# Late chunks of an mLSTM and MoE kernel: a head's three f16 terms on one set of array rows, special scores in quarters, one-hot tables on GpSimd

## Chip, cores and metric

One core of a Trainium2 chip runs the whole kernel. The metric is device microseconds of one execution, the median of several runs. TensorE (PE, with its weight loads as PEld), VectorE (DVE), ScalarE (ACT), GpSimd (POOL) and SyncE (SP, which issues most of the transfers) each work through their own list of instructions in order.

## Reference

Two parts follow each other. The first is an mLSTM over 4 batches, 8 heads, 768 steps, head size 40; the second routes each of the 3072 tokens to one of 8 experts.

```python
for t in range(S):                                   # mLSTM, per batch and head
    C = f * C + i * outer(v_t, k_t);  n = f * n + i * k_t
    y_t = sigmoid(o_t) * (C @ q_t) / max(|n . q_t|, 1)
x = y as (3072 tokens, 8 heads * 40 = 320)
logits = x @ w_gate + modality_bias[modality_id]      # 8 experts
e = argmax(logits);  p = softmax(logits)[e]
out = p * (relu(x @ w1[e]) @ w2[e])                   # 320 -> 1024 -> 320
```

## The kernel before

**Chunks.** The tokens are cut into 24 chunks of 128. Chunks 0 to 21 hold tokens whose output is a product of q with one state of their batch (`S`, 40 rows by 41 columns for each head, the 41st for the denominator); chunks 22 and 23 hold the first 64 steps of each batch, which need their own scores and are called special.

- Chunks 0 to 13 multiply in f32 (`light`, the matmul on L1976): three heads lie under each other on 120 rows of the array, and the state's blocks are masked so that one matmul gives the three heads' 123 columns. Three matmuls make a chunk (3, 3 and 2 heads).
- Chunks 14 to 21 (`light16`, L1985; `SPLIT` = 7 is the first pair that goes this way) do the same in f16. q and S are each split in a high and a low part (`split_q`: ACT makes `qh` on L1983, DVE makes `ql` on L1984; `Sh` and `Sl` likewise), and each group of heads takes three matmuls on L1997: high by high, high by low, low by high. That is nine for a chunk; chunk 16 lies over two batches and has its nine twice, for 64 rows each.
- `special` (L2078): scores in f32 (L2086, 8 matmuls of 128 rows x 64 columns, with a zero-padded `sp` tile that L2470 clears), decay weights `aw` (POOL, POOL, ACT, then DVE on L2095 times the scores), then 16 matmuls with the values (L2101).

**From a chunk to a tile.** `token_rows` normalises two chunks at a time (DVE), multiplies by the reciprocal on POOL (L2034), casts on ACT and makes the low part on DVE; POOL scatters a chunk's rows to `x_s` in DRAM by an indirect transfer (L2045), ordered by modality. 14 tiles are read back transposed by SP (L2140), in the order A0, A1, A2, B0, B1, A3, B2, A4, B3, A5, B4, A6, B5, A7; a tile's transfer waits for the scatters of the chunks that can lie in it. The first three tiles are not read back but picked out of the rows by matmuls with one-hot tables (`sel`, made from positions on L2152).

**Experts.** The tokens are still (one modality, one expert), so two experts' weights, A and B, are loaded in f32 to `stage` buffers and split to f16 high (ACT, L1949) and low (DVE, L1950). A tile takes logits (L2212), a first layer (L2275, and L2283 for the last 64 of 320 rows), relu and split (`hh` on ACT L2263, `hl` on DVE L2264), a second layer (L2320) and a row-wise scatter of the output by POOL (L2341). One odd token is worked out apart: its row is fetched into `zrow` and cast by DVE (L2388).

**Order.** Each piece of work is a task. A list scheduler with a cost for each task and one nudge for each (the strings `PRIO` and `LOADS`) writes out the order on every engine, and each engine then runs strictly in this order. Where the scheduler's plan leaves PE idle for 0.25 us or more before its 60th microsecond, dummy matmuls on a zero tile `zz` are put in (L2524), sized by the planned gap.

Of the kernel before, what the change touches and what calls it, by code (L numbers as in the profile page):

```python
# [1550 lines left out]
SPLIT = 7  # L1551
# [32 lines left out]
    "{+py{Rv{'+{{QOyz{kpggTcnf)v9c_bp{g{][Y]-r,NYHJHC{YvR%%{D&bS[XMBT%5ZcR2{%fq{vtt>TO%pojs{DM7x]=J{[GX{`{acoB_{z:o"
    'Y%W{uhhvX4\\%7%{.%K.ED)2/?T4o%yg%IDCDa@_^t\\]ZyZKtss[ZniF`lgU_dc\\^{b{f{cH%{nu(%hV{%%%%YB?->kQPUX`{{uou{Bm@{zPt{{'
    "oT'{+oeab\\t4S%Z{HJ9Ctmlknn{b5{la{mjks{{ywuvlssxlkm{pRMZd4T*5J(**%<9o=e{z{{X{{yy{{vK{sxvpm{{{{V{pe{{joV%t*e%%:z"
    'mx?B%>=W8[%%h<;RQplqr{d:D]<({]%.W\\ZZig3074,?JGFd,B<o`oT9O6JKxztY{p{`{ep^{nsD{^me_\\b{*qp{ljz-h%=*wfG{2{o{R{{kXx'
    'v{^{sqswtX%ttqn{pi%?gjkuun{W{]wT{YipxSumtx^z[<tkvtseRG%Z@buec)ahrOax]GbT[al]iwmV<AOSGWUv?9%;tnfWEdb<Ca_s0]`N..'
# [63 lines left out]
def still_arm(tc, a, out):  # L1652
# [804 lines left out]
    def chunks(z):  # L2457

        for c in range(done[0], z):
            plan.early = 0.0 if c < 14 else SOON  # L2460
# [212 lines left out]
```

## Time and profile before

| what | value |
|---|---|
| median of three runs | 217.33 us (216.87 to 217.49) |
| the profiled execution: its own time | 218.61 us |
| the profiled execution: span, first to last instruction | 216.8 us |
| mean granted clock of TensorE over the span | 0.989 |

The page gives each engine's busy time over the span; the windows give it by stretch, with the granted clock (1.00 is 2.4 GHz), the DMA engines' busy share and GB/s. The timeline lists neighbouring instructions as one row with a count, and in brackets the idle time ahead of it with what ended it. Matmuls are pipelined: a matmul's listed duration is longer than the distance to the next one, so a piece of work is timed here from its start to the start of what follows.

### The profile page before, as it was taken

How to read it: one execution, taken by the hardware profiler on the slowest of the kernel's cores; microseconds unless marked ns; L12 is line 12 of the kernel's file. 1: busy time of each engine (PE TensorE's matmuls, PEld its weight loads, DVE VectorE, ACT ScalarE, POOL GpSimd, SP SyncE). 2: the span in 40 equal slices, each digit the busy share in tenths (PEclk: the TensorE clock that was granted, in tenths of full speed). 3: DMA queues.
4: the chain of work that ended last, by engine and by line, in shares of the span. 5: the costliest groups of instructions: out<-in, count | busy, mean ns of one | idle time of the engine just before them, and what ended most of it. 6: DMA issues, size and time to landing. Idle time of an engine off the chain costs nothing. (4 is left out here: it accounts for less than half of the span.)

```text
span 216.8 us, 5376 instructions
## 1 busy us (share of the span) xinstructions
PE 206.3 (95%) x2103; PEld 159.6 (74%) x2103; DVE 139.0 (64%) x447; ACT 100.4 (46%) x202; POOL 77.0 (35%) x84
## 2 busy tenths in 40 slices
PE   7899998999999999999999999999999999999970
PEld 2576786878888878878778778787787787767840
DVE  7788975597786936787806596958585159811300
ACT  3797976955655557453425242225432231322310
POOL 5040265643143653546784522330211403032021
PEclk9999999999999999999999999999999999999995
DMA  6989999294444964731637601096000880001010
GB/s 193 362 310 340 326 329 343 97 258 193 92 123 164 120 224 66 183 117 63 176 103 184 104 30 33 33 152 124 33 30 0 300 281 35 30 0 64 3 33 25
DMA packets 27115, 30.76 MB, mean 142 GB/s; under 512 B 19190, under 2 KB 19480, under 8 KB 26824
## 3 DMA queue, kind: packets, MB, share of 16 engines
q1 hardware_dynamic: 24520, 22.06, 36.8%
q0 software_dynamic: 2416, 8.13, 10.7%
q8 instruction: 18, 0.29, 0.6%
q10 hardware_dynamic: 144, 0.13, 0.2%
q14 instruction: 17, 0.14, 0.2%
HBM read 18.57 MB, written 8.22 MB: 124 GB/s over the span
## 5 line engine op out<-in xcount | busy, mean ns | idle before, releaser
L2341 POOL DMA_INDIRECT out<-ob,ois x25 | 24.7, 986 | 70.8 <-ACT ob L2336 17.5
L2320 PEld LDWEIGHTS <-hh 128*128 128x128 f16 (+1 forms) x400 | 37.8, 98 | 16.2 <-ACT hh L2263 1.1
L2264 DVE SCALAR_TENSOR_TENSOR hl<-H,hh 128x512 f16<-128x512 f32 (+2 forms) x40 | 25.8, 648 | 27.8 <-ACT hh L2263 27.7
L2263 ACT ACTIVATE hh<-H 128x512 f16<-128x512 f32 (+2 forms) x40 | 22.3, 565 | 37.5 <-PE H L2275 22.5
L2045 POOL DMA_INDIRECT x_s<-rows,pos_i x24 | 26.2, 1092 | 36.0 <-issue 5.5
L2336 ACT ACTIVATE ob<-O,zs 128x320 f32<-128x320 f32 (+1 forms) x24 | 12.5, 522 | 45.6 <-PE O L2320 32.8
L2320 PE MATMUL O<-w2hA,hh 128*128 128x320 f16 (+1 forms) x104 | 27.8, 300 | 1.0 <-ACT hh L2263 1.0
L2320 PE MATMUL O<-w2lA,hh 128*128 128x320 f16 (+1 forms) x104 | 27.8, 299 | 0.0
L2275 PE MATMUL H<-xt,w1hA 128*128 128x256 f16 (+2 forms) x176 | 26.7, 259 | 0.0
L2320 PE MATMUL O<-w2hB,hh 128*128 128x320 f16 x96 | 26.4, 299 | 0.0
L2320 PE MATMUL O<-w2lB,hh 128*128 128x320 f16 x96 | 26.4, 299 | 0.0
L2275 PE MATMUL H<-xt,w1hB 128*128 128x256 f16 x144 | 24.4, 273 | 0.0
L2320 PEld LDWEIGHTS <-hl 128*128 128x128 f16 (+1 forms) x200 | 18.9, 98 | 7.1
L2275 PEld LDWEIGHTS <-w1hA 128*128 128x128 f16 x224 | 20.3, 98 | 3.5 <-issue 1.2
L2275 PE MATMUL H<-xt,w1lA 128*128 128x256 f16 (+2 forms) x88 | 22.2, 259 | 0.0
L2275 PEld LDWEIGHTS <-w1hB 128*128 128x128 f16 x192 | 18.0, 98 | 3.1 <-issue 0.8
L2275 PE MATMUL H<-xt,w1lB 128*128 128x256 f16 x72 | 19.6, 273 | 0.0
L2034 POOL TENSOR_TENSOR xr<-xr,ab 128x640 f32<-128x640 f32 x11 | 14.5, 1318 | 9.9 <-DVE ab L2017 6.7
L2320 PE MATMUL O<-w2hA,hl 128*128 128x320 f16 (+1 forms) x104 | 16.0, 299 | 0.0
L2019 DVE SCALAR_TENSOR_TENSOR xr<-og,Y 128x320 f32<-128x320 f32 x24 | 11.3, 477 | 7.1 <-PE Y L1997 6.8
L2320 PE MATMUL O<-w2hB,hl 128*128 128x320 f16 x96 | 15.3, 299 | 0.0
L2524 PE MATMUL M<-zz 128*128 128x512 bf16 (+5 forms) x41 | 11.0, 404 | 1.1 <-DVE zz L1792 1.1
(218 smaller groups left out, 397.8 us busy)
## 6 DMA issues: line engine op xcount, KB each, us to landing
qg<-in_ql SPq DMA_DIRECT2D x11, 384.0 KB, 4.4
og<-in_ogl SPq DMA_DIRECT2D x12, 320.0 KB, 5.5
stage<-in_w1s SPq DMA_DIRECT2D x8, 320.0 KB
stage<-in_w SPq DMA_DIRECT2D x8, 320.0 KB, 3.2
stage<-in_w1t SPq DMA_DIRECT2D x1, 1280.0 KB, 8.1
og<-in_w SPq DMA_DIRECT2D x1, 1280.0 KB
kvs<-in_kvs SPq DMA_DIRECT2D x2, 364.5 KB
sp<-in_spq SPq DMA_DIRECT2D x4, 160.0 KB
```

The source lines that it names most:

```text
L2019: dve(320, lambda h=h: v.scalar_tensor_tensor(x4[:, h], og[k][:, h].rearrange("p (h d) -> p h d", h=H), 1.0, y4[h][:, :, 0:D], ALU.add, AL ...
L2034: pool(640, lambda: g_.tensor_tensor(x3, x3, ab.rearrange("p c h o -> p (c h) o").broadcast_to([P, 2 * H, D]), ALU.mult), r=abk, w=xk)
L2045: ins = g_.indirect_dma_start(out=x_s[:, :], out_offset=bass.IndirectOffsetOnAxis(ap=pos_i[:, c:c + 1].bitcast(U32), axis=0), in_=rows[:, ...
L2263: act(g * n, lambda: s_.activation(hh[:, sl, 0:n], hp3, AF.Relu), r=[nb], w=[f"hh{j}{i}" for i in fs])
L2264: dve(g * n, lambda: v.scalar_tensor_tensor(hl[:, sl, 0:n], hp3, 0.0, hh[:, sl, 0:n], ALU.max, ALU.subtract), r=[nb] + [f"hh{j}{i}" for i ...
L2275: t_.matmul(dst, lhsT=w[:, i, ws], rhs=x[:, xb], start=(first and b == 0 and q == 0), stop=(last and b == 1 and q == 2), skip_group_check= ...
L2320: t_.matmul(op[p0:p0 + nr, 0:DM], lhsT=t[:, at[f], o_:o_ + nr], rhs=w[:, f], start=(i < ways), stop=(i >= 24 - ways), skip_group_check=True)
L2336: act(z + 80, lambda op=op, o=o, qc=qc, nr=nr, z=z: s_.mul(obs[o][0:nr, 0:z], op[0:nr, 0:z], facs[0:nr, qc:qc + 1]), r=[no, f"fac{m_}"], w ...
L2341: swdma(164, lambda o=o, qc=qc, nr=nr: disjoint("outf", g_.indirect_dma_start(out=out[:, :], out_offset=bass.IndirectOffsetOnAxis(ap=ois[0 ...
L2524: t_.matmul(bank[b][:, 0:m], lhsT=zz, rhs=zz[:, 0:1].broadcast_to([P, m]), start=True, stop=True, skip_group_check=True)
```

## The change

Chunks 12 to 21 (`SPLIT` = 6) now use one matmul per head. A head's q is laid on 104 + 16 = 120 rows of the array in one f16 tile `qs`: rows 0 to 39 q high, 40 to 63 q high again, 64 to 103 q low, 104 to 119 q high again. Against them stands `SS`, whose rows 0 to 39 and 64 to 103 are the state's high part and rows 40 to 63 and 104 to 119 its low part. q comes already laid out so, one chunk at a time, by a 480 KB transfer (`in_qx`) into `stage` or `qg` buffers. `SS` is put together by 12 transfers from `Sh` and `Sl`, and those are written straight from PSUM without the mask. The scores of the special chunks are 16 matmuls of 64 x 64 on 40 rows, one for each of two row halves and two column halves of the array, into two PSUM banks. Six one-hot tables, and five small or middle operations, go from DVE to GpSimd. `PRIO` and `LOADS` are other strings; a line or two of them is shown.

```diff
-SPLIT = 7
+SPLIT = 6
+STACK = ((0, 40, 0, 0), (40, 64, 0, 1), (64, 104, 0, 0), (104, 120, 24, 1))
 PRIO = (
-    "ou^{%%vT%XKtMF3<&%6U9R{npHOM+G(&%,%%%'3.,GL9<LI[Ah%=%e>H{E%%{{{^F{%D{X6{98{J<q%sxR<{Wu%0{%Qk{%`hGEC'EG%a.?HvD8"
+    "{{*/B%gN%MVN,%O.Yqv)optC{'ZX%otsrxtxu(sjT{wy{{/%%L%%{z{f[o@O{He{OI{NvFEG{K2uFoMJ\\iNr,,{%;QoE{xi{\\`-{_u&%Fu[MXa"
...
+    def load_qx(c):
+        dma(480, lambda: sy.dma_start(qx[c % 3], a["qx"][:, c - 2 * SPLIT]), w=[f"qx{c % 3}"] + qxk[c % 3])
...
-            if S16[b]:
-                hi, lo = S16[b]
-                act(3 * HQ, lambda hi=hi, b=b: s_.mul(hi, Ss[b][0:120], SSC), r=[f"S{b % 3}"], w=[f"S{b}h"])
-                two(3 * HQ, lambda hi=hi, lo=lo, b=b: v.scalar_tensor_tensor(lo, Ss[b][0:120], SSC, hi, ALU.mult, ALU.subtract),
-                    r=[f"S{b % 3}", f"S{b}h"], w=[f"S{b}l"])
+            if pr:
+                hi, lo = (x[:, 3 * j:3 * j + 3] for x in S16)
+                act(3 * HQ, lambda hi=hi, j=j: s_.mul(hi, u3s[j][0:120], SSC), r=[ns[j]], w=[f"S{b}h"])
+                dve(3 * HQ, lambda hi=hi, lo=lo, j=j: v.scalar_tensor_tensor(lo, u3s[j][0:120], SSC, hi, ALU.mult, ALU.subtract),
+                    r=[ns[j], f"S{b}h"], w=[f"S{b}l"])
+        if pr:
+            for p0, p1, d0, x in STACK:
+                for j in range(3):
+                    k0 = D * j + d0
+                    dma(100, lambda p0=p0, p1=p1, x=x, j=j, k0=k0: sy.dma_start(SS[p0:p1, :, DV * j:DV * (j + 1)],
+                                                                             S16[x][k0:k0 + p1 - p0, :, DV * j:DV * (j + 1)]),
+                        r=[f"S{b}{'hl'[x]}" for b in (2, 3)], w=[f"SS{p0}{j}"])
...
-    def split_q(i):
-        q, (hi, lo), k, j = qg[i % 4], q16[i % 2], f"qg{i % 4}", i % 2
-        act(768, lambda: s_.mul(hi, q[0:120], QSC), r=[k], w=[f"qh{j}"])
-        two(768, lambda: v.scalar_tensor_tensor(lo, q[0:120], QSC, hi, ALU.mult, ALU.subtract), r=[k, f"qh{j}"], w=[f"ql{j}"])
-
     def light16(c, n, y):
-        if c % 2 == 0:
-            split_q(c // 2)
-        (qh, ql), i, j = q16[c // 2 % 2], c % 2, c // 2 % 2
+        k = c % 3
+        q, s = qx[k], q16[k]
+        act(1024, lambda: s_.mul(s, q, QSC), r=[f"qx{k}"], w=[f"qs{k}"])
+        two(1024, lambda: v.scalar_tensor_tensor(s[64:104], q[64:104], QSC, s[64:104], ALU.mult, ALU.subtract), r=[f"qx{k}"], w=[f"qs{k}"])

         def mm():
-            for g in range(3):
+            for h in range(H):
                 for p0, p1, b in spans(c):
-                    k, w = (120, HQ) if g < 2 else (80, 2 * DV)
-                    Sh, Sl = S16[b]
-                    for t, (a, z) in enumerate(((qh, Sh), (qh, Sl), (ql, Sh))):
-                        t_.matmul(y[p0:p1, HQ * g:HQ * g + w], lhsT=a[0:k, i, g, p0:p1], rhs=z[0:k, g, 0:w],
-                                  start=(g == 0 and t == 0), stop=(g == 2 and t == 2), skip_group_check=True)
+                    t_.matmul(y[p0:p1, DV * h:DV * h + DV], lhsT=s[:, h, p0:p1],
+                              rhs=SS[:, 3 * b - 6 + h // 3, DV * (h % 3):DV * (h % 3) + DV], start=(h == 0), stop=(h == H - 1),
+                              skip_group_check=True)
...
-    dve(24, lambda: v.tensor_copy(rows[:, :, IDC:IDC + 2].bitcast(I32).rearrange("p c o -> p (c o)"), tok_i), r=["cst"], w=["rowi"])
+    pool(24, lambda: g_.tensor_copy(rows[:, :, IDC:IDC + 2].bitcast(I32).rearrange("p c o -> p (c o)"), tok_i), r=["cst"], w=["rowi"])
...
         def scores():
             for hp in range(NP):
                 for b in range(2):
-                    t_.matmul(sc3[FT * b:FT * b + FT, 2 * hp:2 * hp + 2], lhsT=sp[:, 0, b, hp], rhs=sp[:, 1:3, b, hp],
-                              start=(hp == 0), stop=(hp == NP - 1), skip_group_check=True)
+                    for j in range(2):
+                        rs = slice(64 * j, 64 * j + D)
+                        t_.matmul(scs[j][FT * b:FT * b + FT, hp], lhsT=sp[rs, 0, b, hp], rhs=sp[rs, 1, b, hp],
+                                  start=(hp == 0), stop=(hp == NP - 1), skip_group_check=True)
...
-        dve(512, lambda: v.tensor_tensor(aw, aw, sc3, ALU.mult), r=[n], w=["aw"])
+        aw4 = aw.rearrange("p (h j) t -> p h j t", j=2)
+        for j in range(2):
+            dve(256, lambda j=j: v.tensor_tensor(aw4[:, :, j], aw4[:, :, j], scs[j], ALU.mult), r=[(n, "M0")[j]], w=["aw"])
...
-        two(selw[c] // 4 + 16, lambda: v.tensor_scalar(sels[c], iota_f[:, 0:selw[c]], float(sel0[c]), posf[:, c:c + 1], ALU.add, ALU.is_equal),
+        pool(selw[c], lambda: g_.tensor_scalar(sels[c], iota_f[:, 0:selw[c]], float(sel0[c]), posf[:, c:c + 1], ALU.add, ALU.is_equal),
...
-                load_q(c // 2) if c < 22 else None
+                load_q(c // 2) if c < 2 * SPLIT else [load_qx(x) for x in (c, c + 1)] if c < 22 else None
...
-                dve(800, lambda: v.memset(sp, 0.0), w=["spz"])
```

How the change moves instructions is seen at three places. The first is PE at one late chunk. Before, the nine f16 products of a chunk stand in the first layer of tile B1 (`H`), here the first group of heads and the beginning of the second:

```order
L2275 MATMUL H_64<-xt_108,w1lB 128x256
L1997 LDWEIGHTS qh_83
L1997 MATMUL Y_69<-Sh_87,qh_83 128x123
L1997 LDWEIGHTS qh_83
L1997 MATMUL Y_69<-Sl_88,qh_83 128x123
L1997 LDWEIGHTS ql_84
L1997 MATMUL Y_69<-Sh_87,ql_84 128x123
```

In the changed kernel a chunk is eight such pairs of load and product (here one of them, in tile B1's second layer, `O`; the seven behind it read the same):

```order
L2333 LDWEIGHTS hh0_104
L2333 MATMUL O1_67<-w2lB_96,hh0_104 128x320
L2006 LDWEIGHTS qs2_80
L2006 MATMUL Y0_69<-SS_83,qs2_80 128x41
L2006 LDWEIGHTS qs2_80
```

Each late chunk of one batch goes from nine pairs with 123 or 82 columns to eight with 41, still with a weight load of 128 columns for each.

The second place is ACT where the late chunks begin. Before, it holds one conversion of a pair of chunks (`qh`) and two of states (`Sh`) among the relu outputs `hh` of a tile:

```order
L2263 ACTIVATE hh_112<-H_63 128x512
L2333 ACTIVATE ob_116<-ob_116,zs 64x320
L1983 ACTIVATE qh_81<-qg_77 120x768
L2263 ACTIVATE hh_112<-H_64 128x512
L1876 ACTIVATE Sh_87<-S_120 120x369
L2336 ACTIVATE ob_117<-O_66,zs 128x320
L2263 ACTIVATE hh_112<-H_65 128x512
```

Now three conversions of one chunk each (`qs`, from `stage`, `qg`, `stage`) stand there, one ahead of the two states and two between the `hh`:

```order
L2000 ACTIVATE qs_79<-stage 120x1024
L1972 ACTIVATE og<-og 128x640
L1885 ACTIVATE Sh<-Y_70 120x369
L1885 ACTIVATE Sh<-Y_69 120x369
L2237 ACTIVATE ex_166<-lg_164 128x16
L2349 ACTIVATE ob_110<-O_66,zs 128x320
L2276 ACTIVATE hh_105<-H_63 128x512
L2000 ACTIVATE qs_80<-qg 120x1024
L2276 ACTIVATE hh_105<-H_64 128x512
L2276 ACTIVATE hh_105<-H_65 128x512
L2000 ACTIVATE qs_78<-stage 120x1024
```

So an `hh` now stands directly behind a conversion that needs a transfer of 480 KB of its own.

The third place is POOL ahead of its first multiplication of rows (`xr` by `ab`). Before, that follows the small product `Bs` of the gates:

```order
L1805 AFFINE_SELECT tri_122<-tri_122 128x128
L1831 TENSOR_TENSOR Bs_133<-gs_74,m_130 32x64
L2027 TENSOR_TENSOR xr0_158<-xr0_158,ab0_156 128x320
L2034 TENSOR_TENSOR xr1_159<-xr1_159,ab1_157 128x640
```

Now the copy of token numbers into `rows`, the modality operations and the six one-hot tables stand in between:

```order
L2065 COPY rows_86<-cst_73 128x24
L1933 TENSOR_SCALAR ss_139<-cumx_132 128x2
L1927 TENSOR_TENSOR ge2_143<-ge2_143,cst_73 128x16
...
L1929 TENSOR_TENSOR d2_144<-km2_141 128x2
L2165 TENSOR_SCALAR sel1_158<-iota_f_117,posf_135 128x192
L2165 TENSOR_SCALAR sel0_157<-iota_f_117,posf_135 128x128
L2165 TENSOR_SCALAR sel4_161<-iota_f_117,posf_135 128x128
L2165 TENSOR_SCALAR sel3_160<-iota_f_117,posf_135 128x192
L2165 TENSOR_SCALAR sel2_159<-iota_f_117,posf_135 128x320
L2165 TENSOR_SCALAR sel5_162<-iota_f_117,posf_135 128x128
L2037 TENSOR_TENSOR xr0_151<-xr0_151,ab0_149 128x320
```

What moved is the tables, from DVE to the place right ahead of POOL's first `xr`. Over the whole program the lists differ thus: f16 products of late chunks 81 before, 88 now (16 of them with 64 columns of weights); f32 products of `light` 45 before, 39 now; score matmuls 16 of 128 columns before, 32 of 64 now; dummy matmuls 56 before with 26,695 columns in all, 52 now with 23,625; instructions on DVE 442 and 437, ACT 199 and 194, POOL 84 and 94, SP 110 and 127.

## Rows read from the trace of the kernel before

**Rows 1.** Windows: length; PE, PEld, DVE, ACT, POOL busy; clock; DMA share; GB/s.

```profile
0.00:42.83 42.83, 39.24 (x403) 27.98 (x403) 32.87 (x117) 32.39 (x66) 16.61 (x28) 1.00 0.84 289
42.83:209.85 167.02, 167.02 (x1701) 131.59 (x1700) 105.74 (x331) 67.60 (x136) 59.38 (x56) 1.00 0.41 109
209.85:216.80 6.95, 0.04 (x1) 0.00 (x0) 0.38 (x1) 0.39 (x1) 0.97 (x1) 0.67 0.07 21
```

**Rows 2.** Windows in two shorter stretches, columns as in rows 1.

```profile
10.00:20.00 10.00, 9.92 (x93) 7.70 (x92) 8.39 (x30) 8.48 (x19) 2.34 (x2) 1.00 0.94 323
...
60.00:80.00 20.00, 20.00 (x207) 15.87 (x206) 14.62 (x47) 11.17 (x23) 10.68 (x10) 1.00 0.65 171
```

**Rows 3.** Timeline around 33 us, ACT's two rows and PE's next.

```profile
33.13 0.74 ACT L1949 ACTIVATE w2hB<-stage 128x640 f16<-128x640 f32 x1 [1.63 <-DMA stage<-in_w]
33.77 0.64 ACT L2263 ACTIVATE hh<-H 128x256 f16<-128x256 f32 x2
...
34.19 0.31 PE L2320 MATMUL O<-w2hA,hh 128*128 128x320 f16 x1 [0.97 <-ACT hh L2263]
```

**Rows 4.** Dummy matmuls alone, windows; then PE's timeline at the last five.

```profile
0.00:42.83 42.83, 14.66 (x56) 5.06 (x56) 1.00 0.84 289
...
41.67 1.23 PE L2524 MATMUL Y<-zz 128*128 128x512 bf16 x5
```

**Rows 5.** Timeline of PE, two late chunks: the first product, and what follows.

```profile
83.97 0.22 PE L1997 MATMUL Y<-Sh,qh 120*128 120x123 f16 x1
...
84.74 0.20 PE L1997 MATMUL Y<-Sh,qh 80*128 80x82 f16 x1
...
84.85 0.38 PE L2275 MATMUL H<-xt,w1hA 128*128 128x256 f16 x2
```

**Rows 6.** Timeline of PE, chunk 16 over two batches.

```profile
78.56 0.25 PE L1997 MATMUL Y<-Sh,qh 120*64 120x123 f16 x2
...
79.13 0.45 PE L2320 MATMUL O<-w2hB,hl 128*128 128x320 f16 x2
```

**Rows 7.** Timeline of PE, a pair of f32 chunks.

```profile
60.02 1.46 PE L1976 MATMUL Y<-S,qg 120*128 120x123 f32 x12
61.33 0.30 PE L2320 MATMUL O<-w2hB,hl 128*128 128x320 f16 x1
```

**Rows 8.** Timeline of PE, logits of a tile.

```profile
47.86 0.40 PE L2212 MATMUL M<-wgr,xt 128*128 128x16 f16 x10
...
48.11 0.38 PE L2275 MATMUL H<-xt,w1hB 128*128 128x256 f16 x2
```

**Rows 9.** Timeline of PE, scores and values of special chunks (two records for each f32 matmul).

```profile
109.85 1.09 PE L2086 MATMUL Y<-sp 128*64 128x128 f32 x16
110.88 0.39 PE L2275 MATMUL H<-xt,w1hA 128*128 128x256 f16 x2
...
120.75 1.13 PE L2101 MATMUL Y<-kvs,aw 64*64 64x41 f32 x32
121.82 0.31 PE L2320 MATMUL O<-w2hA,hh 128*128 128x320 f16 x1
```

**Rows 10.** Groups of instructions: count, busy us, mean ns, idle before.

```profile
L1984 DVE SCALAR_TENSOR_TENSOR ql<-qg,qh 120x768 f16<-120x768 f32 x4 | 3.8, 951 | 0.0
L1997 PEld LDWEIGHTS <-qh 120*128 120x128 f16 (+3 forms) x54 | 3.7, 100 | 0.4 <-issue 0.3
...
L1983 ACT ACTIVATE qh<-qg 120x768 f16<-120x768 f32 x4 | 3.4, 838 | 0.0
...
L2152 DVE TENSOR_SCALAR sel<-iota_f,posf 128x128 f16<-128x128 f16 (+2 forms) x6 | 1.3, 261 | 0.0
L2055 DVE COPY rows<-cst 128x24 int32<-128x24 int32 x1 | 1.2, 1243 | 0.0
```

**Rows 11.** Timeline of POOL, its first multiplication of rows.

```profile
12.40 1.03 POOL L2027 TENSOR_TENSOR xr<-xr,ab 128x320 f32<-128x320 f32 x1 [8.15 <-DVE ab L2017]
```

**Rows 12.** Timeline of DVE, the weights of the second special chunk.

```profile
125.08 0.69 DVE L2095 TENSOR_TENSOR aw<-aw,Y 128x512 f32<-128x512 f32 x1 [0.24 <-ACT aw L2094]
```

More of the change, by code (lines that the diff above doesn't have):

```diff
@@ L1584 @@
[L1584 to L1588, printed above, removed]
@@ L1589 @@
-    '{tr{T(:{{{{y{A%8'
+    "{{*/B%gN%MVN,%O.Yqv)optC{'ZX%otsrxtxu(sjT{wy{{/%%L%%{z{f[o@O{He{OI{NvFEG{K2uFoMJ\\iNr,,{%;QoE{xi{\\`-{_u&%Fu[MXa"
+    "tap%{tb2`_M/luGGav>l;fBkqFoG/=;:i&'&Y6==``<`Po%+146]1(/O5&*xVC,ikOFIOIE4uR32R%df6Z^C%)?%664.R:%KL6HF%<]M=J:C3F"
+    "AI=6<g+%6<iD3McB.%27LJ]'%1Mh[a%+;,%/)N555%%%-'*492>R=%%D+57%-:L%-3c;%S_{K*RFE[MB.9@BvR_p]JzDM+:VTSIz%RRGCCxYu;"
+    "5U).0%;*KWHVIP;WkOr8%+UvY&&K7%%%%%C?Af{o`gBbFi]j%h;ZF43h[C)GYgg_SDOgEo>fP@;jQ)2hM-,'*'dTQ)0(T`KJ[p-[-@9&y/&%N'"
+    "-',%6(d5]aBTG1*LKLIM+L^`QI>ThP.N%%%%&;\\8M;J{{]w{zo?OU{Hr%emupzOZMLx{{bnkI;DxK=?s_<'SLTT{ezxNUzws,uLthEW:,YH%%,"
@@ new lines @@
+    'X^&5g%9B<6V8O9svwu%X>I{yxwt&9wPtthynJDRW9BN>UPJ4VM;@2GE6C3<Z,?@@?89%B<<=p%;S&y%%[%8Yq6WrcgwOo%Z%@N%9+&G2M[>3S>'
+    "3]+=..+2:(%6)'(N%-N*(&%[H`EIEFCA.\\+h%*_H*Q&uftUtOPL{i_Oq%\\E8Qm?b%ctsE{+dKX;\\{64]]<>Xj<9lz797O11&fXV.O+(3S(+%%g"
+    "zzTpmoYZ_{fiebp{{fR{l{u*={{6`(PE9edomScJB'KrpBKM:3;K4'[P0/Wo.1Us,*''R:AKe53430N90LEBEUatB9=%7U5(%b=QZuMLITJHG{"
+    'FEMbDBS><YJ,JH\\R;W=TG%{XUTTnG\\Q%u*8-&%%U]Hc_>ISYXQ&*(L%{2=1?{pnqn864[X.<P&%o%%{X@%H)%DCNNBIR0.?U/d+a([+UUus=po'
+    "*s]64i{y%Q%+%ZUUa=X0+]25{_1%\\c5')'D@\\E@<699F?9C?+ECG%?:A'L5b:H1C7D.gM[?51db->?=*&%U%XVz+F%4+)2z*V.UA]w.uarp14]"
@@ L1590 @@
+    "[Yjh`%-+%_QE/%PN*JX@+BB'-H%BZRPU&+NLPINK%3,"
 )
 LOADS = (
-    "@<)@7%])E6<U(fNNIX,X=V1jk-M1)%k(%{L@%I%{JA1+z%5'aRC0*=%I%@%@iI%=3(4Nr8VD+[.FJN_<Y3JW@DeY559%9m{M%_.%C5.VD,o6@Y"
-    '9{`@p\\L\\a%{%/Q+ROI{>'
+    "Q3%&8%q_sc>{.%*Vh,^`%89E.J%%6%N&2&'?%[R*g+%=.%;6x/E5%%7'C1%J.(hQK;]^UY4%C=%A>4oebz9eG?.\\%*g)<wG%<%-%%ZBV6V[)GE"
+    '),<5+y4YU+PC=:{CHP(o4%&8:8+MJWu6%9@7%'
 )
@@ L1723, in still_arm @@
     kvs = [tl([P, 9 * D + 9 * DV], F32, f"kvs{i}") for i in range(2)]
-    qg = [tl([P, 2, 3, P], F32, f"qg{i}") for i in range(4)]
-    q16 = [[tl([120, 2, 3, P], F16, f"q{n}{i}") for n in "hl"] for i in range(2)]
-    S16 = [None] * B if SPLIT > 10 else [None] + [[tl([120, 3, HQ], F16, f"S{n}{b}") for n in "hl"] for b in range(1, B)]
+    qgs = tl([P, 4, 6 * P], F32, "qg")
+    qg = [qgs[:, i].rearrange("p (c g t) -> p c g t", c=2, g=3) for i in range(4)]
+    q16 = [tl([120, H, P], F16, f"qs{i}") for i in range(3)]
+    S16 = [tl([120, 6, HQ], F16, f"S{n}") for n in "hl"]
+    SS = tl([120, 6, HQ], F16, "SS")
     ogs = tl([P, NOG * 2 * DM], F32, "og")
@@ L1735, in still_arm @@
     stage = [stg[:, WP * i:WP * i + WP] for i in range(8)]
+    qx = [f[0:120, 0:H * P].rearrange("p (h t) -> p h t", h=H)
+          for f in (stg, stg[:, 2 * WP:], qgs[:, 2:4].rearrange("p i n -> p (i n)"))]
+    qxk = (["stage0", "stage1"], ["stage2", "stage3"], ["qg2", "qg3"])
     W = {}
@@ L2079, in special @@
         n = f"Y{pr}"
-        sc = y = bank[n]
-        sc3 = sc.rearrange("p (h t) -> p h t", h=H)
+        y = bank[n]
+        scs = [bank[m][:, 0:NP * FT].rearrange("p (h t) -> p h t", h=NP) for m in (n, "M0")]
         def scores():
@@ L2384, in odd_row @@
         dma(1311, lambda: sy.dma_start(stg[:, 0:NFC * DM], a["w1t"][ds(regs["F"], 1)].rearrange("a p f -> (a p) f")), r=["regF"],
-            w=[f"stage{i}" for i in range(4)], lat=3.0)
+            w=[f"stage{i}" for i in range(4)] + ["qx0", "qx1"], lat=3.0)
         dma(1311, lambda: sy.dma_start(ogs[:, 0:NFC * DM], a["w2"][ds(regs["F"], 1)].rearrange("a p f -> (a p) f")), r=["regF"],
@@ L2615, in _layout_still @@
     qt = q.transpose(0, 2, 1, 3)[b_, t_]
-    ql = np.zeros((P, 22, 3, P), np.float32)
+    n32 = 2 * SPLIT
+    ql = np.zeros((P, n32, 3, P), np.float32)
     for h in range(H):
         g, j = divmod(h, 3)
-        ql[D * j:D * (j + 1), :, g] = qt[0:22, :, h].transpose(2, 0, 1)
+        ql[D * j:D * (j + 1), :, g] = qt[0:n32, :, h].transpose(2, 0, 1)
+    rows_of = np.concatenate([d0 + np.arange(p1 - p0) for p0, p1, d0, _ in STACK])
+    qx = qt[n32:22].transpose(3, 0, 2, 1)[rows_of]
     ogl = o.transpose(0, 2, 1, 3)[b_, t_].reshape(NC, P, DM).transpose(1, 0, 2)
```

31 lines of the change are left out of this document (13 added, 18 removed).

## The prediction

> **What bounds the kernel now.** I read the windows first. From 42.83 us to 209.85 us PE is busy for all of 167.02 us at clock 1.00 [rows 1]. VectorE, ScalarE and GpSimd have 61, 99 and 108 us free in that stretch, and the DMA engines are busy 0.41 of it. So from 42.83 us on, what counts is the work on PE's list, and any work taken off it comes off the end. After it come 6.95 us of last output, scatter and end, which the change leaves alone.
>
> The first 42.83 us are another stage. There the chain from loads through weights, states and gathered rows sets the pace: DMA is busy 0.94 of 10 to 20 us, VectorE and ScalarE 8.39 and 8.48 of 10 [rows 2], and of PE's 39.24 busy us [rows 1] 14.66 are dummy matmuls [rows 4]. PE's busy time says nothing there. One place shows what a wait looks like under the dummies: ScalarE stands 1.63 us at a weight conversion whose load is late, the relu outputs behind it start late, and PE's second layer is idle for 0.97 us [rows 3].
>
> **What the stacked chunks are worth.** Two f16 chunks run from 83.97 to 84.85 us, 0.44 us a chunk [rows 5]. There are seven of these: 3.08 us. Chunk 16, in two halves, takes 79.13 - 78.56 = 0.57 us [rows 6]. The f32 pair, 12 and 13, of which there is one fewer, takes 61.33 - 60.02 = 1.31 us [rows 7]. Together 4.96 us.
>
> In their place stand 88 pairs of a weight load and a product with 41 columns. No row shows this shape; two stand on either side. Logits, 10 pairs with full loads of 128 columns and 16 moving columns, take 48.11 - 47.86 = 0.25 us, 25 ns a pair [rows 8]. The 82-column products of a late chunk take 84.85 - 84.74 = 0.11 us for three, 37 ns a pair [rows 5]. By the lower row 88 pairs cost 2.2 us, by the upper 3.2 us. I take 2.2: from 123 to 82 columns the distance falls with the columns (0.44 us less 0.11 is 0.33 us for six, 55 ns), and half of 37 is already below 25. The gain is 4.96 - 2.2 = **2.76 us**, between 1.8 and 3.0 (the upper end if the 16 half-width pairs of chunk 16 run two at a time, 0.2 us less).
>
> **Scores.** Eight matmuls with 128 columns take 110.88 - 109.85 = 1.03 us, twice in the program. The nearest row to a 64 x 64 quarter is that of the values: 16 matmuls of 64 x 64 with 41 columns, two at a time, take 121.82 - 120.75 = 1.07 us, 0.134 us a pair [rows 9]. If four quarters run together, 16 matmuls are four steps, 0.54 us, and 0.98 us is gained over both; if only the column halves run together, it is eight steps, 1.07 us, and the gain is nil. The quarters differ in rows, columns and PSUM bank, so I take the first, a little under it: **0.9 us**, bounds 0 and 1.0.
>
> **The early stretch.** The plan wants 23,625 dummy columns instead of 26,695: 3,070 fewer. The last five are busy for 1.23 us right up to the full stretch; over all 56, 14.66 us [rows 4] for 26,695 columns is 0.55 ns a column, so that the fall is worth at most 1.7 us. But fewer dummies are only fewer if the chain below is faster. For it speaks that VectorE, close to full there, loses six tables (1.3 us) and the copy of token numbers (1.2 us) [rows 10]. Against it, the same DMA share has to bring the same weights. I take **1.0 us**. Upper bound: all of the 2.5 us that VectorE loses there comes back, with a little rest 2.7. Lower bound: another conversion stands for its load for 1.6 us, as in [rows 3], and nothing hides it: -1.6.
>
> **What is added off PE.**
> - ScalarE: ten conversions of 1024 elements. The row has 838 ns for 768 [rows 10], so at most 1.12 us each, 11.2 us, for 3.4 us removed. In 60 to 80 us ScalarE is busy 11.17 of 20 [rows 2], so there is room for the 7.8 us; without it each conversion would hold a relu by its own 1.1 us.
> - VectorE: ten low parts at up to 951 x 1024/768 = 1.27 us, 12.7 us, less 3.8, 1.3 and 1.2 us [rows 10]: some 6 us against 5.4 us free in 60 to 80 us and 61 in the whole stretch [rows 1, 2]. This is the tightest cover.
> - GpSimd: the tables have 1088 columns in all. By its only row near, 1.03 us for a product of 320 columns, they cost up to 3.5 us, and they stand ahead of the first `xr`. It was idle for 8.15 us ahead of that [rows 11], so they fit unless positions come later than some 8 us.
> - DMA: ten loads of 480 KB for five of 384, 2.9 MB more, and 12 short copies into `SS`. At 0.41 busy in the long stretch [rows 1] that is hidden. On SP the copies stand around the transposed load of tile B1. In PE's list some 180 products lie between those of the states and the first stacked chunk; at 167.02 us for 1701, 0.098 us each [rows 1], that is 17 us, enough even if each copy held SP for 0.6 us (7 us) and each conversion ahead of the states cost its 1.1 us. I cost them at nothing.
>
> The special chunks come about one tile later in PE's list. Behind the second values stand about 150 products, 15 us at the same 0.098, until the logits of the next gathered tile; scatter and gather have room. From the first values to the second stand 16 quarters and 58 products, 5.7 us. Before, the weights for the second were ready at 125.08 + 0.69 = 125.77 us [rows 12], 3.95 us after the first values' end at 121.82 [rows 9], so this fits by 1.7 us.
>
> **Sum.** 2.76 + 0.9 + 1.0 = 4.66 us. The profiled execution took 218.61 us (span 216.8, 1.8 around it) and would take 213.95; it is 1.28 us above the median of the runs shown, so the median goes from 217.33 to **212.7 us**.
>
> **A rule weighed.** The pairs at the logits follow each other by 25 ns although each loads 128 columns [rows 8], and the loads of a late chunk last 100 ns each [rows 10] while its pairs are 37 to 55 ns apart: several loads are under way at once. The Trainium skill ("TensorE: Matmul & The Clock Gate", section "LDWEIGHTS (loading the stationary operand)") states a load time of the number of columns over 1.2 in ns, 107 ns for 128, whatever the rows; by that as the distance, an estimate, 88 loads would be 9.4 us instead of 2.2. The trace has nearly that duration, but not as a distance.
>
> **Rivals.**
> 1. *The gain is partly eaten by new waits on ScalarE.* Relu outputs stand directly behind conversions whose 480 KB must have come; at 33 us such a wait cost PE 0.97 us [rows 3]. For it: three conversions lie within ten ScalarE instructions, and their buffers are free only when weights are split. Against it: DMA is at 0.65 in 60 to 80 us [rows 2]. If three of ten hold PE: 212.7 + 2.9 = 215.6, or with two 214.6. Chance 0.18.
> 2. *Slower: most conversions hold PE.* The same mechanism, place and price. Gain and loss balance at 4.66 / 0.97, just under five of the ten conversions; from six on it is slower: 218.5. The one ScalarE queue would have to be late almost every time, with 99 us free. Chance 0.07.
> 3. *Loads run one at a time.* With 100 ns a pair [rows 10] the 88 pairs cost 8.8 us, 3.8 more than the 4.96 removed; with 0.9 and 1.0 gained the time is 219.3. Against it stand the 25 ns at the logits [rows 8]. Chance 0.02.
> 4. *The change does less than it says.* Products at 37 ns, row halves of the scores one after the other, early stretch unchanged: 217.33 - 1.8 = 215.5. For the scores no row shows row halves in f32 at once. Chance 0.08.
> 5. *The early stretch gives back more.* If VectorE alone sets it: 217.33 - 2.76 - 0.9 - 2.7 = 211.0. Chance 0.08.
>
> The forecast itself has 0.57.
>
> **How the numbers follow.** A measurement of this kernel can tell about 0.3%, 0.65 us, from no change: 216.7 to 218.0. The low end takes the best of each term, 217.33 - 3.0 - 1.0 - 2.7 = 210.6. The high end is that of rivals 1 and 4, 215.6. Outside lie rivals 2 and 3 and about a tenth of the others. Faster: the forecast, 4 and 5 and nearly all of 1, less a little for the early stretch's worse end, 0.87. Within 0.3%: 0.04, from 1 and 2 about five waits. Slower: 0.09.
>
> **What would show it right or wrong.** The profile of the changed kernel should show a stacked chunk from its first product to the following one in 0.2 us (0.30 says the upper row; 0.8 says loads one at a time); a special's scores in 0.55 us (1.05 says the row halves don't run together); PE without gaps from about 42 us to its end; and ScalarE's idle time ahead of `qs` not followed by idle time of PE. PE gaps released by `hh` behind a `qs`, or by `SS`, would make it wrong; so would a full stretch that begins later than 43.5 us. If the end of the dummies comes at 40 us or earlier, rival 5 has it.

## The result, and the profile after

The changed kernel takes 219.99 us (median of 16 runs, 218.31 to 221.15), the kernel before beside it 217.35 us (16 runs, 216.66 to 218.55); the ratio is 1.011 (95% interval 1.0083 to 1.0138). Here and below a time is the median of all runs, and a ratio leaves disturbed runs out. Forecast were 212.7 us and a range of 210.6 to 215.6. The profiled execution has a span of 218.6 us, against 216.8.

Windows of the changed kernel over all (columns as in [rows 1]):

```profile
0.00:60.00 60.00, 57.08 (x592) 42.57 (x593) 48.10 (x168) 44.52 (x90) 28.23 (x44) 1.00 0.84 266
60.00:100.00 40.00, 34.13 (x374) 26.61 (x372) 29.55 (x76) 23.39 (x41) 18.69 (x15) 0.96 0.70 179
100.00:211.90 111.90, 111.90 (x1165) 87.21 (x1162) 68.67 (x200) 38.34 (x77) 36.17 (x34) 1.00 0.34 95
211.90:218.60 6.70, 0.02 (x1) 0.00 (x0) 0.38 (x1) 0.39 (x1) 0.97 (x1) 0.82 0.07 22
```

PE's busy time has fallen from 206.30 us (the sum of [rows 1]) to 203.14 us (the same window over the whole span): that is the gain. But where PE was full from 42.83 us on, it is now idle for 40.00 - 34.13 = 5.87 us between 60 and 100 us. The view of PE's waits names them (in total, times, longest):

```profile
PE H L2288 <- DMA xt<-x_s: 2.2, 1, 2.2
PE Y L2006 <- DMA SS<-Sl: 2.0, 1, 2.0
PE M L2225 <- DMA xt<-x_s: 1.5, 1, 1.5
```

The three are the first layer of tile A3 (its transposed load came late), the first stacked chunks (the copies into `SS`), and the logits of tile B1 (transposed load). SP's timeline tells why, for the second and third:

```profile
49.68 3.49 SPq L1892 DMA_DIRECT2D SS<-Sh  x4
53.27 0.79 SPq L1892 DMA_DIRECT2D SS<-Sl  x1
...
57.05 1.63 SPq L1892 DMA_DIRECT2D SS<-Sl  x2
58.91 1.91 SPq L2153 DMA_TRANSPOSE xt<-x_s  x1
60.88 0.57 SPq L2154 DMA_DIRECT2D zs<-x_s  x1
61.52 0.66 SPq L1892 DMA_DIRECT2D SS<-Sl  x1
62.28 0.51 SPq L2483 DMA_DIRECT2D stage<-in_gll  x1
62.89 0.82 SPq L1786 DMA_DIRECT2D stage<-in_qx  x2
63.76 0.62 SPq L1892 DMA_DIRECT2D SS<-Sl  x1
```

The copies of 8 to 19 KB hold SP for 0.6 to 1.0 us each. Ten of them and one gate load stand ahead of B1's transposed load and keep it until 58.91 us; PE wants B1 at 61.40. The twelfth copy goes out at 63.76 us behind two loads of 480 KB and lets PE's chunk go at 70.75, seven microseconds later; in between (64 to 70 us) the DMA engines are busy for 0.96. PE's timeline at this chunk:

```profile
68.50 0.21 PE L2006 MATMUL Y<-SS,qs 120*128 120x41 f16 x2
70.75 0.53 PE L2006 MATMUL Y<-SS,qs 120*128 120x41 f16 x14 [2.03 <-DMA SS<-Sl]
```

The third wait comes behind the second, by a tie in the order. Timelines of VectorE, GpSimd, SP and PE of the changed kernel, in this order:

```profile
67.99 0.90 DVE L2048 TENSOR_TENSOR rows<-xr,rows 128x128 f16<-128x128 f32 x2
71.31 0.17 DVE L2022 TENSOR_REDUCE ab<-Y 128x8 f32<-128x8 f32 x1 [2.42 <-PE Y L2006]
...
71.98 0.17 DVE L2026 TENSOR_SCALAR ab<-ab 128x16 f32<-128x16 f32 x1
...
72.25 2.01 POOL L2055 DMA_INDIRECT x_s<-rows,pos_i  x1 [3.87 <-ACT qs L2000]
...
73.44 0.33 SPq L1786 DMA_DIRECT2D stage<-in_qx  x1
78.69 1.37 SPq L2153 DMA_TRANSPOSE xt<-x_s  x1
...
82.93 0.50 PE L2288 MATMUL H<-xt,w1hA 128*128 128x256 f16 x2 [2.22 <-DMA xt<-x_s]
```

The kernel ties each scatter of GpSimd to a VectorE instruction that the plan has just before it, to space the scatters out. The scatter of chunk 10, whose rows are ready by about 68.9 us, is tied to a step behind the stacked chunk's output, and so goes at 72.25. The bracket names ScalarE's `qs`, which ends at 72.17 us, as VectorE's step ends at 72.15; the scatter reads neither, and it is run 3 below that shows the tie. A load of 480 KB follows it out at 73.44, and the transposed load of A3, which needs that scatter landed, starts only at 78.69.

After the 2.22 us without work, TensorE's clock falls as well; windows of two microseconds:

```profile
82.00:84.00 2.00, 1.07 (x6) 0.81 (x6) 1.40 (x2) 0.81 (x2) 1.69 (x2) 0.76 1.06 304
84.00:86.00 2.00, 2.00 (x20) 1.45 (x20) 0.12 (x1) 0.00 (x0) 1.55 (x2) 0.50 0.92 214
86.00:88.00 2.00, 2.00 (x29) 1.51 (x26) 0.37 (x1) 1.66 (x3) 0.00 (x0) 0.88 1.01 293
```

0.50 is 1.2 GHz. In 84 to 88 us alone this costs 2 x 0.50 + 2 x 0.12 = 1.2 us of work at 2.4 GHz, and it is counted as busy.

What the change was to bring is there. PE's timeline of the changed kernel, a stacked chunk and the first special chunk's scores (sixteen matmuls, two records each; the first and the last):

```profile
74.71 0.36 PE L2006 MATMUL Y<-SS,qs 120*128 120x41 f16 x8
74.92 0.30 PE L2333 MATMUL O<-w2hB,hh 128*128 128x320 f16 x1
...
136.44 0.27 PE L2097 MATMUL Y<-sp 40*64 40x64 f32 x1
...
137.07 0.45 PE L2333 MATMUL O<-w2hB,hl 128*128 128x320 f16 x2
```

A stacked chunk takes 0.21 us (0.44 in [rows 5]), the scores 0.63 us (1.03 in [rows 9]). And the groups of added work on ScalarE and GpSimd:

```profile
L2165 POOL TENSOR_SCALAR sel<-iota_f,posf 128x128 f16<-128x128 f16 (+2 forms) x6 | 5.3, 898 | 0.5 <-DVE pbig L2386 0.5
...
L2000 ACT ACTIVATE qs<-stage 120x1024 f16<-120x1024 f32 x7 | 7.4, 1056 | 3.9 <-PE Y L2006 2.6 <-DMA stage<-in_qx 1.2
```

### The profile page after: what moved, and what is told of

The parts are those of the page before. It is cut to its first block, busy times and chain, and to the rows that moved or that the text cites. A ratio compares the mean times of both kernels' runs of the same rounds, so it can differ in the third digit from the quotient of the medians.

```text
span 218.6 us, 5475 instructions
## 1 busy us (share of the span) xinstructions
PE 203.1 (93%) x2126; PEld 156.4 (72%) x2126; DVE 146.7 (67%) x442; ACT 106.7 (49%) x207; POOL 84.1 (38%) x94
## 5 line engine op out<-in xcount | busy, mean ns | idle before, releaser
L2055 POOL DMA_INDIRECT x_s<-rows,pos_i x24 | 28.1, 1172 | 38.7 <-ACT qs L2000 7.3
L2288 PE MATMUL H<-xt,w1hA 128*128 128x256 f16 (+2 forms) x176 | 27.7, 266 | 2.2 <-DMA xt<-x_s 2.2
L2288 PE MATMUL H<-xt,w1lA 128*128 128x256 f16 (+2 forms) x88 | 22.8, 266 | 0.0
L2333 PE MATMUL O<-w2hB,hl 128*128 128x320 f16 x96 | 15.8, 299 | 0.0
L1972 ACT ACTIVATE og<-og 128x640 f32<-128x640 f32 x12 | 8.7, 734 | 8.1 <-DMA og<-in_ogl 8.0
```

The lines of the kernel that those rows point to most:

```text
L1972: act(640, lambda: s_.activation(t, t, AF.Tanh, scale=0.5), w=[k])
L2055: ins = g_.indirect_dma_start(out=x_s[:, :], out_offset=bass.IndirectOffsetOnAxis(ap=pos_i[:, c:c + 1].bitcast(U32), axis=0), in_=rows[:, ...
L2288: t_.matmul(dst, lhsT=w[:, i, ws], rhs=x[:, xb], start=(first and b == 0 and q == 0), stop=(last and b == 1 and q == 2), skip_group_check= ...
L2333: t_.matmul(op[p0:p0 + nr, 0:DM], lhsT=t[:, at[f], o_:o_ + nr], rhs=w[:, f], start=(i < ways), stop=(i >= 24 - ways), skip_group_check=True)
```

## The experiments

Theory A: the copies into `SS` hold SP and land late, the waits follow from that and from the tie. Theory B: the added transfers are too much for the DMA engines between 60 and 70 us, whoever issues them and in whatever order. All versions are of the changed kernel, in its planned order, if not said otherwise. Times are medians; ratios are to the kernel before on the same chip.

**1. Copies issued by GpSimd.**

```diff
-    sy.dma_start(SS[p0:p1, :, DV * j:DV * (j + 1)], ...)
+    g_.dma_start(SS[p0:p1, :, DV * j:DV * (j + 1)], ...)
```

> The 12 copies into SS are issued by GpSimd instead of SP, everything else in the order of the changed kernel. Theory A (the copies hold SP for 0.75 us each, so that tile B1's transposed load and the last copy come late): SP is free again, B1's logits wait under 0.3 us instead of 1.51, SS is there before the first stacked chunk, the time falls by 4 us or more to 216 or less. Theory B (the transfers themselves are too much for the DMA engines between 60 and 70 us, whoever issues them): waits of the same 5 to 6 us remain, 219 to 220.5.

Measured: 219.31 us, ratio 1.0047 (1.0002 to 1.0092). PE's waits in this version:

```profile
PE Y L2006 <- DMA SS<-Sl: 2.6, 1, 2.6
...
PE M L2225 <- DMA xt<-x_s: 0.4, 1, 0.4
```

With SP free, B1's transposed load goes at 53.21 us, and that wait is gone (the 0.4 us is a later tile's). The wait for `SS` stays: the twelfth copy is still issued late (64.18 us, its place in the order) behind three loads of 480 KB, the last two of them issued at 61.58 and 61.95 us. So SP's time explains one wait, and what is left is the copies' place among the loads. Neither expectation held whole: the time is B's and not A's 216 or less, but of the 5 to 6 us of waits that B wanted the first is gone. The interval of the ratio touches the changed kernel's, so no gain in time is shown.

**2. SP's list sorted anew.** The same twelve copies by SP: four, the gate load, B1's transposed load, the other eight, then the loads of `gll` and chunks 15 to 17.

```diff
+    line = ["SS641", "SS642", "SS640", "SS01", "og3", "x4", "ids4", "SS401", "SS00", "SS1040", "SS02", "SS400", "SS402", "SS1041",
+            "SS1042", "gl"]
...
+    for k, i in zip(sps[at:], [now[names.index(x)] for x in line] + [i for i, x in zip(now, names) if x not in line]):
+        order[k] = i
```

> Only SP's list is sorted anew in one place: four copies, the gate load, B1's transposed load and its ids, the eight other copies, and only then the loads of gll and of chunks 15 to 17. Theory A: PE's waits of 1.51 (logits), 2.03 (SS) and 2.22 us (transposed load of A3) and the lower clock behind them go, the time is 213 to 215. Theory B (transfers as such): the last copies land as late as before, near 70 us, and the time stays above 218.

Measured: 217.24 us, ratio 0.9957 (0.9909 to 1.0006). The two waits are gone, and so is B's forecast of a late landing; but A's 213 to 215 was wrong. SP's and PE's timelines show what the place alone does:

```profile
61.09 2.97 SPq L1892 DMA_DIRECT2D SS<-Sl  x4
...
66.73 0.57 PE L2006 MATMUL Y<-SS,qs 120*128 120x41 f16 x16
```

The last copy leaves SP at 64.06 us, hardly earlier than the 64.38 us of the changed kernel, but ahead of the two loads, and PE's sixteen products at 66.73 us wait for nothing. So it is what stands ahead of the last copy, and not SP's time for the copies, that made `SS` late. PE's and ScalarE's timelines show what came instead:

```profile
71.39 0.31 PE L2333 MATMUL O<-w2hB,hh 128*128 128x320 f16 x1 [1.03 <-ACT hh L2276]
...
74.36 0.31 PE L2333 MATMUL O<-w2hB,hh 128*128 128x320 f16 x1 [1.21 <-ACT hh L2276]
```

```profile
69.80 1.06 ACT L2000 ACTIVATE qs<-stage 120x1024 f16<-120x1024 f32 x1 [2.92 <-DMA stage<-in_qx]
70.76 0.58 ACT L2276 ACTIVATE hh<-H 128x512 f16<-128x512 f32 x1
72.76 1.06 ACT L2000 ACTIVATE qs<-stage 120x1024 f16<-120x1024 f32 x1 [1.42 <-DMA stage<-in_qx]
73.72 0.58 ACT L2276 ACTIVATE hh<-O 128x512 f16<-128x512 f32 x1
```

The loads that now stand behind the copies are late, ScalarE waits at the conversion, and the relu output behind it holds PE: the pattern of [rows 3], twice, at 1.0 and 1.2 us.

**3. No tie of the scatters.**

```diff
-        if t["eng"] == "POOL" and t["kb"] is not None and steps and plan.start[i] < plan.UNTIL:
+        if t["eng"] == "POOL" and t["kb"] is not None and steps and plan.start[i] < 45.0:
```

> GpSimd's scatters from 45 us of the plan on are no longer tied to a VectorE instruction (they have to wait only for their own data). If the 2.22 us before A3's first layer follow from the SS wait by way of that tie, the scatter of chunk 10 goes out near 70 us instead of 72.25, A3's transposed load comes 2 us or more earlier, the wait and the lower clock behind it shrink, and the time falls by 2 to 3 us to 217 to 218, with the 1.51 and the 2.03 still there. If the tie doesn't matter, the time stays within 0.5 us of the changed kernel's.

Measured: 217.1 us, ratio 0.9938 (0.9893 to 0.9982), 2.9 us less than the changed kernel. PE's waits:

```profile
PE M L2225 <- DMA xt<-x_s: 1.9, 1, 1.9
PE Y L2006 <- DMA SS<-Sl: 1.6, 1, 1.6
```

GpSimd's scatter of chunk 10 and SP's transposed load of A3, 72.25 and 78.69 us in the changed kernel:

```profile
69.94 0.98 POOL L2055 DMA_INDIRECT x_s<-rows,pos_i  x1 [1.28 <-ACT hh L2276]
...
73.91 1.37 SPq L2153 DMA_TRANSPOSE xt<-x_s  x1
```

The first two waits are there as before, A3's is gone, and in 80 to 100 us PE is busy for all 20 us at clock 1.00. So the third wait and the fall of the clock come by way of the tie.

**4. The same on the kernel before**, as a control: that line alone.

> The kernel before without the tie of its scatters from 45 us of the plan on, to see whether the tie costs there too. PE has no wait from 42.83 us on in the trace of before, so nothing can be gained behind it: 217.0 to 217.7. If 1 us or more is gained here, the gain of the versions without the tie isn't the change's.

Measured: 218.04 us, ratio 1.0015 (0.998 to 1.0049); the kernel before takes 217.6 us on that chip. Taking the tie away gains nothing there.

**5. Long rows.** The states stored head by head, so that a copy moves 492-byte rows.

```diff
-    SS = tl([120, 6, HQ], F16, "SS")
+    SS = tl([120, 3, 6, DV], F16, "SS")
...
-    sy.dma_start(SS[p0:p1, :, DV * j:DV * (j + 1)], S16[x][k0:k0 + p1 - p0, :, DV * j:DV * (j + 1)])
+    sy.dma_start(SS[p0:p1, j], S16[x][k0:k0 + p1 - p0, j])
```

> The changed kernel with the states stored head by head, so that each of the 12 copies into SS moves rows of 492 bytes (40, 24 or 16 of them) instead of six pieces of 82 bytes for each row; the order of all engines is the changed kernel's. (ScalarE and VectorE write each state in three instructions instead of one.) Theory A, in the form that the number of short pieces is what costs: a copy holds SP for 0.3 to 0.45 us instead of 0.78, the last copy lands before its chunk, PE's waits of 1.51 and 2.03 us go or fall under 0.5 us together, the time is 214.5 to 216.5. Rival: SP's time for a copy doesn't depend on the pieces and stays at 0.7 us or more; nothing changes, 219 to 220.5.

Measured: 219.49 us, ratio 1.0102 (1.0036 to 1.0168). A copy of 40 rows (in the view of the line: least, median, most ns) costs nearly as much as the changed kernel's 767, 782 and 1007:

```profile
L1894 SPq DMA_DIRECT2D SS<-Sh x6: 706/724/912, 50.0 to 55.5; - x6
```

The rival was right: the number of short pieces is not what SP's time hangs on. That form of theory A fell. The time is the rival's too. PE's wait for `SS` is 1.1 us here instead of 2.0, the one for B1's tile 2.4 us instead of 1.5.

**6. Long rows and no tie.**

> As the run with long rows, and GpSimd's scatters from 45 us of the plan on are not tied to VectorE. If with SS in time the tie no longer costs anything, it equals the run with long rows within 0.6 us; if the tie also delays scatters by itself, it is 1 us or more faster, 213 to 215.

Measured: 215.64 us, ratio 0.9927 (0.9898 to 0.9956), 3.9 us less than with the tie. That is the second branch, a little above its 213 to 215. The waits for B1 and `SS` are 1.5 and 0.7 us here. In run 5 `SS` was not in time, so this pair does not tell what the tie costs without that wait; run 8 does.

**7. Copies split, and ahead of the loads.** The six copies of low parts by GpSimd, the six of high parts by SP, all ahead of gate load, transposed load and the loads of chunks 15 to 17; no tie.

```diff
-    sy.dma_start(SS[p0:p1, :, DV * j:DV * (j + 1)], ...)
+    (g_ if x else sy).dma_start(SS[p0:p1, :, DV * j:DV * (j + 1)], ...)
...
+    line = ["SS641", "SS642", "SS640", "SS01", "SS401", "SS00", "SS1040", "SS02", "SS400", "SS402", "SS1041", "SS1042", "og3", "x4",
+            "ids4", "gl", "qx1"]
```

> Short pieces as in the changed kernel, but the six copies of the low parts go by GpSimd and the six of the high parts by SP, all ahead of the gate load, B1's transposed load and the loads of gll and chunks 15 to 17 (chunk 16 first); scatters not tied. Theory A: no wait of PE for SS or for B1's tile, loads of chunks 15 to 17 go out near 57 to 62 us instead of 63 to 65, no relu waits behind them: 213 to 215. If the wait only moves to the conversions, as in the run with the copies first (1.0 and 1.2 us before hh), 215.5 to 217.5.

Measured: **213.86 us** (213.47 to 214.28), ratio 0.9837 (0.9818 to 0.9855): 1.6% under the kernel before, and below the changed kernel too. Its window from 60 to 100 us, and what is left of PE's waits behind 50 us:

```profile
60.00:100.00 40.00, 39.24 (x444) 31.27 (x443) 35.17 (x91) 25.35 (x46) 19.69 (x18) 1.00 0.78 189
```

```profile
PE O L2333 <- ACT hh L2276: 0.9, 1, 0.9
PE Y L2006 <- DVE xr L2029: 0.6, 1, 0.6
```

The DMA share is 0.78 here, higher than the 0.70 of the changed kernel in the same stretch, with PE nearly full. Theory B is about the middle of it; windows from 64 to 70 us, the changed kernel and this version:

```profile
64.00:70.00 6.00, 4.71 (x55) 3.77 (x53) 4.74 (x14) 2.46 (x5) 3.27 (x3) 1.00 0.96 229
64.00:70.00 6.00, 6.00 (x80) 5.09 (x78) 4.75 (x12) 2.57 (x4) 4.25 (x4) 1.00 0.95 237
```

The DMA engines are as busy in both, and PE stands 1.29 us in one and not at all in the other. That speaks against theory B. One part of the expectation was wrong: the loads of chunks 15 to 17 go out at 62.6 us and not earlier.

**8. The same with the tie.**

> The best version so far (copies split over SP and GpSimd, all ahead of the loads) with the tie of GpSimd's scatters to VectorE put back. If copies and tie are each a cost of their own, it stands between 214.5 and 217, and the wait for A3's transposed load is back in part; if the tie only passes on the wait for SS, it equals the version without the tie, 213.5 to 214.3; if the tie is the whole of it, it is near 219.

Measured: 215.49 us, ratio 0.9916 (0.9884 to 0.9948), 1.6 us more than without. The wait is at a transposed load again, now that of the tile behind A3 (PE goes on at 90.30 us); A3's own is 0.3 us:

```profile
PE M L2225 <- DMA xt<-x_s: 1.3, 1, 1.3
```

So the copies' issue and place are worth 219.99 - 215.49 = 4.5 us with the tie and 217.1 - 213.86 = 3.2 us without; the tie is worth 2.9 us with the copies late and 1.6 us with them in time. These versions ran on several chips; by the ratios, each to the kernel before on its own chip, the four figures are 4.2, 2.2, 3.7 and 1.7 us. So the tie also costs something where PE does not wait for `SS`.

**9. Each copy twice.**

```diff
-    lambda ...: sy.dma_start(SS[...], S16[x][...])
+    lambda ...: [sy.dma_start(SS[...], S16[x][...]) for _ in range(2)][1]
```

> The changed kernel with each of the 12 copies into SS issued twice, both by SP. If SP's time for a copy is what delays B1's transposed load and the last copy, SP is held 7 to 8 us longer ahead of B1's load, PE's wait at B1's logits grows from 1.5 to 7 us or more, and the time is 225 or more. If SP has slack there, it stays within 1 us of the changed kernel's.

Measured: 247.47 us, ratio 1.1392. The dose is larger than meant, since the second copy of a pair also waits until the first has landed. SP's and PE's timelines:

```profile
82.69 1.37 SPq L2154 DMA_TRANSPOSE xt<-x_s  x1
...
86.22 0.44 PE L2226 MATMUL M<-wgr,xt 128*128 128x16 f16 x10 [25.30 <-DMA xt<-x_s]
```

B1's transposed load is 82.69 - 58.91 = 23.8 us later, and PE's wait at B1's logits grows by 25.3 - 1.5 = 23.8 us. What delays SP there reaches PE one to one.

**10. Quarters alone, in the kernel before.** The scores' hunk of the diff, and a second bank among what the scores write.

> The kernel before with the scores in quarters alone, in its own order. Theory A: the quarters gain what the records show, about 0.8 us of 217.3. Rival: row halves or the second bank bring a wait elsewhere, and nothing or less than 0.3 us is gained.

Measured: 218.68 us, ratio 1.0053 (1.0004 to 1.0101). This is inconclusive: the second bank in the dependences made the scheduler write another order, with waits of PE for `hl` (0.8 us) and for `sp` (0.5 us) that the kernel before doesn't have.

**11. Old scores in the best version (7).**

```diff
-    t_.matmul(scs[j][FT * b:FT * b + FT, hp], lhsT=sp[rs, 0, b, hp], rhs=sp[rs, 1, b, hp], ...)
+    t_.matmul(sc3[FT * b:FT * b + FT, 2 * hp:2 * hp + 2], lhsT=sp[:, 0, b, hp], rhs=sp[:, 1:3, b, hp], ...)
```

> The best version so far with the scores of the special chunks as before (16 matmuls of 128 columns, a zeroed tile, cleared by GpSimd behind its seventh multiplication of rows). If the quarters are worth what the records say, it is 0.6 to 1.0 us slower than that version, 214.5 to 214.9; if the product of PE's list isn't what counts there, no difference.

Measured: 214.16 us, ratio 0.9831 (0.9791 to 0.9871), beside 0.9837 of version 7. The intervals lie over each other. The quarters' 0.7 to 0.8 us is seen in PE's rows; whether it reaches the end is not shown.

**12. Tables on GpSimd, in the kernel before.** Six one-hot tables and the copy of token numbers on GpSimd at their old place in the order.

> The kernel before with the six one-hot tables and the copy of token numbers on GpSimd, at their old place in the order. If VectorE sets the pace of the early stretch, the stretch before 43 us shrinks: the order and the dummies are fixed, so at most the 0.97 us wait near 33 us and part of the other early waits go, 0 to 1.5 us faster. Rival: GpSimd is slower at the tables (up to 3.5 us) and its first multiplication of rows comes late: 0 to 2 us slower.

Measured: 217.16 us, ratio 0.9994 (0.9977 to 1.0011): no difference. Moving these seven alone brings nothing.

## Why the prediction was wrong, point by point

- **The step that failed** is the one on the copies into `SS`: "I cost them at nothing." It compared 12 x 0.6 us of SP with the time to the first stacked chunk. That room was there: 21 us from the states' products (47.49 us) to the first stacked one (68.50), for 9.45 us of SP, 0.6 to 1.0 us a copy. What failed is that only the sum was compared; the step left out two things that the order decides: B1's transposed load is queued behind ten of them on SP (1.51 us of PE), and the last copy is queued behind two loads of 480 KB (2.03 us). Runs 1, 2 and 9 show both apart. PE's gap released by `SS` is also one of the signs that the prediction named for being wrong.
- **A link that the prediction did not have**: the tie of the scatters to VectorE. It carried the wait for `SS` to tile A3 (2.22 us, and the slower clock behind it, 1.2 us or more), as run 3 shows. By run 4 it costs nothing in the kernel before; by run 8 it costs 1.6 us in the new order even with `SS` in time, so it is not only a carrier of that wait.
- **Stacked chunks**: right. Nine chunks at 0.21 us and chunk 16 near 0.4 us make 2.3 us for 4.96; 2.7 us gained in PE's list, forecast 2.76. That 128-column loads follow each other at some 26 ns held, so the rival with loads one at a time is out.
- **Scores**: right in kind. The first special chunk's take 0.63 us instead of 0.54, the second's 0.70 us (141.28 to 141.98) with the last products of values among them: 0.7 to 0.8 us gained in PE's list for both, forecast 0.9.
- **Early stretch**: near in size by these two profiles, the reason not shown. Dummies fell from 14.66 to 14.09 us of busy time, and PE's idle time up to 60 us from 60.00 - 56.41 to 60.00 - 57.08, 3.59 to 2.92 us: 1.2 us together, forecast 1.0. Windows of the kernel before, and of the dummies in the changed one:

```profile
0.00:60.00 60.00, 56.41 (x581) 41.76 (x582) 46.82 (x165) 42.53 (x86) 22.57 (x33) 1.00 0.78 257
...
0.00:42.83 42.83, 14.09 (x52) 4.87 (x52) 1.00 0.92 304
```

  The idle time varies from profile to profile, though: up to 43 us it is 1.40 to 2.95 us in the ten with the new early order, 3.59 and 3.63 us in the two with the old one, and 2.73 us in run 12, whose time is that of the kernel before. So the size is no better known than to about a microsecond. That VectorE's lost tables bring it is not borne out by run 12's time; what in the new order does stays open.
- **Off PE**: a conversion takes 1.06 us (forecast at most 1.12). The tables take GpSimd 5.3 us instead of at most 3.5, without a wait of PE that names them. ScalarE has five instructions more, and not five fewer as the list of differences has it: the pages count 202 before and 207 after.
- **Rivals**: the mechanism of 1 and 2, relu outputs held behind conversions, does not appear in the changed kernel; it comes up in run 2, once the copies stand ahead of the loads, at 1.0 and 1.2 us, where 0.97 was forecast for one. Rival 3 named 219.3 us, near the measured time, but its mechanism is not there: that is a coincidence.
- **The account**: PE idle -0.67 us up to 60 us and +5.87 us from 60 to 100 us, busy -3.16 us (the gains less the slower clock), the tail -0.2 us: +1.84 us, and the spans differ by 1.8. (The medians differ by 2.6 us: the profiled execution of before was 1.28 us above its median, that of after 0.37.) With most of the waits removed, version 7 is 3.5 us under the kernel before; forecast were 4.66, and behind 50 us 1.5 us of waits are left in it.

## What to carry to other kernels

Copies of a few kilobytes inside the chip's memory are not free on the queue that issues them: count them by their number, ask what stands behind them on that queue and which large loads stand ahead of the last of them. A wait of two microseconds need not stay where it is: what is tied or queued behind it, here a scatter by a pacing rule, was late for a tile 12 us further on. And when a change's gain is in an engine's list and its time is not, the idle time by stretch and the waits by name find it in two views.

## What the runs showed of the hardware

- SP's time for one of the copies is 0.78 us (40 rows, 240 pieces of 82 bytes) and 0.72 us (40 rows of 492 bytes), while the loads of 480 KB with 120 rows of 4096 bytes take 0.33 to 0.57 us. Neither bytes nor pieces explain that; what does was not tried.
- A copy of 8 KB issued behind two loads of 480 KB let its reader go 7.0 us after its issue (changed kernel); in run 2 the last such copy left SP at 64.06 us, ahead of these loads, and its reader went at 66.73 us without a wait.
- The two row halves and two column halves of f32 scores run together: four records start within 0.02 us, eight such fours follow at about 0.06 us, and all 16 matmuls take 0.63 us.
- TensorE's clock fell to 0.50 after one gap of 2.22 us in the changed kernel, and after one of 2.60 us in run 1; in run 3, with gaps of 1.9 and 1.6 us, and in run 5, with one of 2.4 us, it stayed at 1.00 around them. The length of the gap alone doesn't tell.
